# Small steps of each variance's root on ScalarE, VectorE or GpSimd, under a new written-out order

## The chip, the cores and the metric

The kernel runs on one core of one Trainium2 chip. The metric is the time of one execution in device microseconds. Five engines work side by side and run their own instructions in order: TensorE (PE) multiplies matrices into PSUM, VectorE (DVE) and ScalarE (ACT) work on SBUF and PSUM, GpSimd (POOL) works on SBUF only, and SyncE (SP) issues transfers that 16 DMA engines carry out. They meet through semaphores.

## The reference

Four layers act on one sequence of 2048 rows of 512 numbers, an attention layer (A) and a mixer (B), twice each with the same weights:

```python
x = x + A(layernorm(x), wqkv, wo)
x = x + B(layernorm(x), w1, w2, w3, w4)
x = x + A(layernorm(x), wqkv, wo)
x = x + B(layernorm(x), w1, w2, w3, w4)

def layernorm(x):                       # eps = 1e-5
    m, v = mean(x), var(x)              # over the 512 columns
    return (x - m) / sqrt(v + eps)
```

`A` has 32 heads of 16 columns; each row attends to 8 rows: itself and those 2, 4, ... 14 rows before it, with a softmax over the 8. `B` computes `h = gelu(layernorm(x) @ w1)`, shifts the four quarters of the columns of `h` by +1, -1, +2 and -2 rows, sets `x1 = x + shifted @ w2`, and returns `x1 + gelu(layernorm(x1) @ w3) @ w4` with a hidden width of 1792. Every layer norm needs, for each row, the reciprocal of a root of the variance: `r = (v + eps) ** -0.5`, and the shift `-m * r`.

## The kernel before, in words

**Tiles.** 128 rows are one tile, four tiles one block of 512 rows, and there are four blocks. Two layer pairs (attention and mixer) times four blocks make eight steps, n = 0 to 7. A step has stages, each a function that adds operations to a graph: `p1_quarters` and `p1_stream` (norm of x, product with wqkv, keys and values out to HBM; line 846), `p2` (attention; line 1021), `p3` (product with wo, residual, norm, product with w1, gelu; line 1148), `p4` (product with w2, norm of x1; line 1278) and `p5` (products with w3 and w4; line 1341). Products are made from pairs of f16 numbers (a high and a low half), as three f16 matmuls each, so a 128x512 product over 512 columns is a group of twelve matmuls. The low halves (`f<-f,f` in the profile, "turn" functions at lines 684 and 696) are made by VectorE or GpSimd, then a transposing transfer puts the tile in place for the next product.

**The root.** The sum of a tile's rows comes out of the instruction that makes the tile. `sq_dev` (line 651, ScalarE) squares the deviations and sums them into `ss`, 128 numbers, one a row. `power` (line 657) then issues three instructions on GpSimd, each on 128x1 numbers, through `stepped` (line 667): a first step `ve = ss * c1 + c2`, the power `r = ve ** -0.5`, and a last step `nb = (tot * c) * r`. In the profile all of these carry the name `small`: the first and the last are GpSimd's TENSOR_SCALAR `small<-small`, the power is its TENSOR_TENSOR `small<-small,nhalf`. `normed` (line 675) then applies `x * r + nb` as one ScalarE activation (in some tiles GpSimd does it); it appears as `f<-x,small`, `f<-f,small` and the like. `p1_norm` (line 750) has a form of the same three steps for the first block, and `p3` one with four steps (lines 1200 to 1205) on the roots of four tiles at once. In all there are 92 calls of `power`, 4 tiles of the first block, and 8 roots over four tiles.

**The order.** Nothing is left to the order in which the functions run. Every operation of the graph gets its place from a printed list, `PLACES` (line 56), and its engine, where it has more than one alternative, from a printed list `OTHER` (line 205). `plan` (line 278) goes through the operations by place, keeps along the way an estimate of the time at which each engine, transfer lane and buffer comes free, and gives each new tile the buffer that by this estimate is free first. Each engine then executes its instructions strictly in that order (line 354, which is why all rows of the profile name L354).

Of the kernel before, what the change touches and what calls it, by code (L numbers as in the profile page):

```python
# [12 lines left out]
ALU = mybir.AluOpType  # L13
# [214 lines left out]
class Graph:  # L228
# [3 lines left out]
    def __call__(self, key, alts, r=(), w=(), after=(), xfer=0.0, late=0.0):  # L232
# [34 lines left out]
        return o  # L267


LAT, LAT_PE, LAT_SP, LAT_DMA, LEAD, TABLE, COLD = 0.06, 0.35, 0.15, 1.5, 0.85, 1.3, 1.0  # L270
TAIL = (0.165, 0.085, 0.115, 0.0, 0.0)
FREE = (6.5, 1.0, 0.72, 1.2, 0.72)
LANES = 8
GRANT, HELD, SMALL = 0.14, 0.4, ("tiny", "root")
BY_DMA = {"p1": 1, "p2": 1, "p3": 1, "p4": 0}


# [1182 lines left out]
```

## Time and profile before

| | |
|---|---|
| median of 3 runs | 1149.2 us (1148.75 to 1150.22) |
| the profiled execution | 1149.52 us |
| its span, first to last instruction | 1147.7 us |
| mean granted TensorE clock | 0.995 |
| TensorE busy | 98% of the span |
| VectorE busy | 77% |
| ScalarE busy | 54% |
| GpSimd busy | 43% |

A row of the profile names the source line, the engine, the operation, output and inputs by the program's names, partitions and elements, and the count. In a timeline the first two numbers are start and length in microseconds, and brackets hold the idle time of that engine before the instruction and what ended it. In a list of groups the two numbers behind the first bar are the total in microseconds and the mean in nanoseconds of one. The busy time of TensorE includes matmuls that run at a lower granted clock.

### The profile page before, as it was taken

The page shows a single profiled execution, that of the slowest core. Times are in us where ns is not written, and L with a number is a line of the kernel's source. Part 1 is how long each engine was busy: PE and PEld are TensorE (multiplying, and loading weights), DVE is VectorE, ACT ScalarE, POOL GpSimd, SP SyncE. Part 2 cuts the span into 40 slices and gives each one's busy share as a digit, 9 for nine tenths or more (in the row PEclk, how much of TensorE's full clock was granted, in tenths as well). Part 3 has the DMA queues.
Part 4 walks back from the last instruction along what each step waited for, and adds up shares of the span by engine and source line. Part 5 has one row for each costly group of instructions (what it writes and reads, how often), then busy time and mean ns, then how long its engine had stood idle before and what let it go on. Part 6 is the DMA issues. An engine that isn't in the chain of part 4 may idle for free.

```text
span 1147.7 us, 15205 instructions
## 1 busy us (share of the span) xinstructions
PE 1121.6 (98%) x5236; PEld 526.5 (46%) x5236; DVE 880.8 (77%) x914; ACT 617.6 (54%) x1077; POOL 489.9 (43%) x619
## 2 busy tenths in 40 slices
PE   8999998998999999999999899999999999999998
PEld 6554444443444444444444344444444444444544
DVE  3999999988998998887889787777877989423212
ACT  4975884257754476365554556463545545545322
POOL 4656584156423455255535323444545342324000
PEclk9999999999999999999999899999999999999999
DMA  7789999998988579974488649884767567434323
GB/s 221 192 215 230 244 260 252 239 219 221 241 230 205 116 193 204 243 195 119 108 218 201 158 112 243 197 211 126 170 175 208 154 152 188 110 83 83 102 83 101
DMA packets 247101, 207.16 MB, mean 180 GB/s; under 512 B 134344, under 2 KB 188616, under 8 KB 247024
## 3 DMA queue, kind: packets, MB, share of 16 engines
q1 hardware_dynamic: 245408, 204.42, 71.2%
q10 hardware_dynamic: 1616, 1.77, 0.5%
q8 instruction: 41, 0.67, 0.3%
q14 instruction: 36, 0.29, 0.1%
HBM read 132.64 MB, written 37.87 MB: 149 GB/s over the span
## 4 chain that ended last, share of the span: by engine, by line
PE 55%; DVE 18%; POOL 8%; issue 7%; ACT 6%; DMA 5%; SPq 1%; POOLq 0%; DVEq 0%; ACTq 0%
PE mm L354 38%; PE acc L354 17%; DVE prod L354 10%; POOL small L354 4%; DVE L L354 3%; ACT f L354 2%; ACT junk L354 1%; SPq L354 1%; DMA kv<-kv_d 1%; DVE x L354 1%; POOL f L354 1%; DVE f L354 1%; DVE mx L354 1%; DVE g L354 1%; DMA w<-in_A_x_dram 1%
## 5 line engine op out<-in xcount | busy, mean ns | idle before, releaser
L354 PE MATMUL acc<-w,g 128*128 128x512 f16 (+1 forms) x1260 | 308.3, 393 | 2.0 <-DVE g L354 0.5
L354 PE MATMUL mm<-nT,w 128*128 128x512 f16 (+1 forms) x1344 | 293.5, 372 | 2.1 <-DVE g L354 1.1
L354 PE MATMUL mm<-wq_hl,xt 128*128 128x512 f16 x1008 | 230.4, 384 | 10.3 <-ACT f L354 3.4
L354 PEld LDWEIGHTS <-w 128*128 128x128 f16 x1512 | 141.2, 98 | 158.6 <-issue 7.3
L354 POOL TENSOR_SCALAR small<-small 128x1 f32<-128x1 f32 (+1 forms) x204 | 120.2, 590 | 158.2 <-ACT junk L354 147.0
L354 ACT ACTIVATE mm<-mm,s_w 128x512 f32<-128x512 f32 (+1 forms) x144 | 90.0, 627 | 174.3 <-PE mm L354 173.9
L354 PEld LDWEIGHTS <-g 128*128 128x128 f16 x1176 | 114.5, 98 | 140.4 <-DVE g L354 2.7
L354 DVE TENSOR_TENSOR prod<-kv,L 128x2048 f32<-128x2048 f32 x64 | 150.0, 2344 | 14.6 <-POOL o L354 10.3
L354 PEld LDWEIGHTS <-xt 128*128 128x128 f16 x1008 | 99.2, 99 | 132.3 <-issue 14.7
L354 DVE TENSOR_REDUCE L<-prod 128x128 f32<-128x2048 f32 x64 | 146.0, 2282 | 1.1
L354 DVE TENSOR_TENSOR prod<-kv,q 128x2048 f32<-128x2048 f32 x58 | 139.6, 2407 | 4.2 <-DMA kv<-kv_d 2.6
L354 DVE TENSOR_TENSOR prod<-prod 128x1024 f32<-128x1024 f32 (+1 forms) x114 | 121.5, 1068 | 5.3 <-ACT prod L354 2.8
L354 DVE SCALAR_TENSOR_TENSOR g<-mm,c_g,g 128x512 f16<-128x512 f32 x56 | 41.5, 746 | 78.2 <-ACT g L354 78.1
L354 PE MATMUL mm<-nT,w_hl 128*128 128x512 f16 x384 | 87.2, 380 | 1.8 <-DVE mx L354 1.8
L354 PE MATMUL mm<-w_hl,h 128*128 128x512 f16 x384 | 86.1, 379 | 0.4 <-POOL h L354 0.2
L354 POOL TENSOR_TENSOR g<-f,g 128x512 f16<-128x512 f32 x31 | 48.6, 1569 | 84.7 <-ACT f L354 42.0
L354 PE MATMUL mm<-wo_hl,oT 128*128 128x512 f16 x336 | 74.2, 379 | 0.0
L354 POOL TENSOR_TENSOR small<-small,nhalf 128x1 f32<-128x1 f32 (+1 forms) x104 | 71.1, 684 | 6.3
L354 POOL TENSOR_TENSOR prod<-prod 128x512 f32<-128x512 f32 x17 | 23.9, 1408 | 104.6 <-DVE prod L354 104.6
L354 ACT ACTIVATE g<-mm,c_g 128x512 f16<-128x512 f32 x98 | 66.5, 684 | 2.0
L354 PEld LDWEIGHTS <-oT 128*128 128x128 f16 x426 | 41.4, 98 | 50.4 <-DVE oT L354 1.2
L354 PEld LDWEIGHTS <-w_hl 128*128 128x128 f16 x384 | 37.6, 99 | 48.0 <-issue 4.2
(196 smaller groups left out, 1253.3 us busy)
## 6 DMA issues: line engine op xcount, KB each, us to landing
w<-w SPq DMA_DIRECT2D x210, 256.0 KB
kv<-kv_d SPq DMA_DIRECT2D x112, 352.0 KB
kv_d<-ev SPq DMA_DIRECT2D x112, 128.0 KB
w<-in_B_w_dram SPq DMA_DIRECT2D x42, 256.0 KB
q_d<-ev SPq DMA_DIRECT2D x28, 256.0 KB
w<-g SPq DMA_DIRECT2D x28, 256.0 KB
q<-q_d SPq DMA_DIRECT2D x28, 256.0 KB
x<-x SPq DMA_DIRECT2D x26, 256.0 KB
```

What stands on the lines that cost most here:

```text
L354: i = f(*a, **k).ins
```

## The change

`stepped` is gone. The three steps of `power` become four operations, and three of these have two alternatives each:

- a new step `tc = tot * C0` (GpSimd or ScalarE), which needs only the sum of the tile;
- the first step `ve = ss * c1 + c2` through a new function `affine` (ScalarE with a bias tile, or GpSimd);
- the power, always on GpSimd;
- the last step `nb = tc * r` (ScalarE or GpSimd).

The form in `p1_norm` gets the same alternatives for its first and last step, without `tc`. The root over four tiles in `p3` has three steps instead of four: the first on ScalarE or GpSimd, the power on GpSimd, the last, which now uses the four `tc`, on GpSimd or VectorE. Three constants for the bias are written by VectorE at the start, and the tile of small numbers grows from 288 to 336 columns.

Both printed lists are new. `OTHER` names 311 operations instead of 137, `PLACES` orders 3597 operations instead of 3513. `plan` no longer estimates times: it goes through the operations by place and gives each new tile the buffer that was returned first in that order.

```diff
 def plan(ops, slots):
-    free, latest = list(FREE), {}
-    lane, lanes = 0, [0.0] * LANES
-    pool = {k: [(0.0, j) for j in range(len(v))] for k, v in slots.items()}
+    pool = {k: list(range(len(v))) for k, v in slots.items()}
+    order = sorted(ops, key=lambda o: o.key)
...
-                got = min(pool[b.kind])
-                pool[b.kind].remove(got)
-                begin, b.slot = max(begin, got[0]), got[1]
+                b.slot = pool[b.kind].pop(0)
...
-                pool[b.kind].append((latest[b] + LAT, b.slot))
+                pool[b.kind].append(b.slot)
...
+    epss = const.tile([P, 3], F32, name="epss")
+    eps_of = {c: epss[:, k:k + 1] for k, c in enumerate((EPS, EPS / SN ** 2, EPS ** 2 / SN ** 2))}
+    for c, t in eps_of.items():
+        V.memset(t, c)
...
-    def power(key, ss, ve, r, i, c1, c2, tot, c, nb, k=None, j=None):
+    def power(key, ss, ve, r, i, c1, c2, tot, tc, nb, k=None, j=None):
         s, k, j = slice(i, i + 1), i if k is None else k, i if j is None else j
-        stepped(key, [
-            (0.21, lambda: G.tensor_scalar(ve.t[:, s], ss.t[:, j:j + 1], c1, c2, ALU.mult, ALU.add), [(ss, j)], [(ve, i)]),
-            (0.58, lambda: G.tensor_tensor(r.t[:, s], ve.t[:, s], nhalf[:, :1], ALU.pow), [(ve, i)], [(r, i)]),
-            (0.27, lambda: G.tensor_scalar(nb.t[:, s], tot.t[:, k:k + 1], r.t[:, s], c, ALU.mult, ALU.mult),
-             [(tot, k), (r, i)], [(nb, i)])])
-    def stepped(key, steps):
-        for k, (d, fn, r, w) in enumerate(steps):
-            gp(key, d, fn, r, w, cls="root" if k == len(steps) - 1 else "tiny")
+        op(key, [(POOL, 0.21, lambda: G.tensor_scalar(tc.t[:, s], tot.t[:, k:k + 1], C0, None, ALU.mult), "tiny"),
+                 (ACT, 0.25, lambda: A.activation(tc.t[:, s], tot.t[:, k:k + 1], AF.Copy, scale=C0), None)],
+           [(tot, k)], [(tc, i)])
+        affine(key, 1, ve, s, lambda: ss.t[:, j:j + 1], c1, c2, [(ss, j)], [(ve, i)])
+        gp(key, 0.58, lambda: G.tensor_tensor(r.t[:, s], ve.t[:, s], nhalf[:, :1], ALU.pow), [(ve, i)], [(r, i)], cls="tiny")
+        op(key, [(ACT, 0.25, lambda: A.activation(nb.t[:, s], tc.t[:, s], AF.Copy, scale=r.t[:, s]), None),
+                 (POOL, 0.27, lambda: G.tensor_scalar(nb.t[:, s], tc.t[:, s], r.t[:, s], None, ALU.mult), "root")],
+           [(tc, i), (r, i)], [(nb, i)])
+    def affine(key, n, ve, s, src, c1, c2, r, w):
+        bias = eps_of[c2]
+        op(key, [(ACT, 0.25, lambda: A.activation(ve.t[:, s], src(), AF.Identity, bias=bias, scale=c1), None),
+                 (POOL, 0.21, lambda: G.tensor_scalar(ve.t[:, s], src(), c1, c2, ALU.mult, ALU.add), "tiny")], r, w)
...
-        stepped(key + 0.2, [
-            (0.21, lambda: G.tensor_scalar(ve1.t[:, s4], ss.t[:, s4], C1, EPS, ALU.mult, ALU.add), [(ss, tiles)], [ve1]),
-            (1.04, lambda: G.tensor_tensor(r1.t[:, s4], ve1.t[:, s4], nhalf, ALU.pow), [ve1], [(r1, tiles)]),
-            (0.22, lambda: G.tensor_tensor(nb1.t[:, s4], sums.t[:, s4], r1.t[:, s4], ALU.mult),
-             [(sums, tiles), (r1, tiles)], [(nb1, tiles)]),
-            (0.23, lambda: G.tensor_scalar(nb1.t[:, s4], nb1.t[:, s4], C0, None, ALU.mult), [], [(nb1, tiles)])])
+        affine(key + 0.2, NT, ve1, s4, lambda: ss.t[:, s4], C1, EPS, [(ss, tiles)], [ve1])
+        gp(key + 0.2, 1.04, lambda: G.tensor_tensor(r1.t[:, s4], ve1.t[:, s4], nhalf, ALU.pow), [ve1], [(r1, tiles)], cls="tiny")
+        op(key + 0.2, [(POOL, 0.22, lambda: G.tensor_tensor(nb1.t[:, s4], tc.t[:, s4], r1.t[:, s4], ALU.mult), "root"),
+                       (DVE, 0.17, lambda: V.tensor_mul(nb1.t[:, s4], tc.t[:, s4], r1.t[:, s4]), None)],
+           [(tc, tiles), (r1, tiles)], [(nb1, tiles)])
```

The numbers such as 0.21 or 0.58 in these lines are the estimates that `plan` used before; in the changed kernel nothing reads them.

More of the change, by code (lines that the diff above doesn't have):

```diff
@@ L267, in __call__ @@
         return o
[L270 to L274, printed above, removed]
 BY_DMA = {"p1": 1, "p2": 1, "p3": 1, "p4": 0}
 def plan(ops, slots):
-    free, latest = list(FREE), {}
-    lane, lanes = 0, [0.0] * LANES
-    pool = {k: [(0.0, j) for j in range(len(v))] for k, v in slots.items()}
-    for o in ops:
+    pool = {k: list(range(len(v))) for k, v in slots.items()}
@@ L285, in plan @@
+    order = sorted(ops, key=lambda o: o.key)
+    for o in order:
         for kind, j in o.lend:
-            pool[kind].remove((0.0, j))
-    dma_free, port, wide, table, order = 0.0, 0.0, 0.0, None, []
-    for o in sorted(ops, key=lambda o: o.key):
+            pool[kind].remove(j)
+    for o in order:
         assert o.n == 0, "an operation stands before one that it needs"
-        e, d, o.fn, cls = o.alts[OTHER.get(o.seq, 0)]
-        begin = o.est
+        o.fn = o.alts[OTHER.get(o.seq, 0)][2]
@@ L292, in plan @@
         for b in o.touch:
             if b.slot is None:
-                got = min(pool[b.kind])
-                pool[b.kind].remove(got)
-                begin, b.slot = max(begin, got[0]), got[1]
+                b.slot = pool[b.kind].pop(0)
                 b.t = slots[b.kind][b.slot]
-        begin = max(begin, free[e])
-        if o.xfer:
-            begin = max(begin, *(lanes[(lane + k) % LANES] for k in range(o.parts)))
-            free[e] = begin + d
-            dma_free = max(dma_free, begin + d + LEAD) + o.xfer
-            o.end = dma_free + LAT_DMA + o.late
-            for k in range(o.parts):
-                lanes[lane] = o.end
-                lane = (lane + 1) % LANES
-        else:
-            if e == ACT and cls is not None and cls != table:
-                table = cls
-                d += TABLE
-            if e == POOL:
-                if begin < port:
-                    begin = max(begin, port - GRANT)
-                wide = max(wide, begin) if cls in SMALL else begin + d - GRANT
-            elif cls == "lock":
-                begin = max(begin, wide)
-                port = begin + d
-            if e == PE and begin - free[PE] > COLD and begin > 20.0:
-                d += min(begin - free[PE] - COLD, 2.5)
-            o.end = begin + d + (TAIL[PE] if e == PE else 0.0)
-            free[e] = o.end - TAIL[e]
-            if cls == "root":
-                o.end += HELD
@@ L324, in plan @@
-        order.append(o)
         for s in o.succ:
-            g = s.alts[0][0]
-            s.est = max(s.est, o.end + (LAT if e == g else LAT_PE if g == PE else LAT_SP if g == SP else LAT))
             s.n -= 1
         for kind, j in o.lend:
-            pool[kind].append((o.end + LAT, j))
+            pool[kind].append(j)
         for b in o.touch:
-            latest[b] = max(latest.get(b, 0.0), o.end)
             b.left -= 1
             if b.left == 0:
-                pool[b.kind].append((latest[b] + LAT, b.slot))
+                pool[b.kind].append(b.slot)
@@ L414, in keep @@
         return Buf(None, const.tile(shape, dt, name=name))
-    small, used = const.tile([P, 288], F32, name="small"), [0]
+    small, used = const.tile([P, 336], F32, name="small"), [0]
     def few(n):
         used[0] += n
-        assert used[0] <= 288
+        assert used[0] <= 336
         return Buf(None, small[:, used[0] - n:used[0]])
@@ L647, in tile_mixer @@
     stat = {ph: [[few(n) for k in range(SC)] for j in range(m)]
-            for ph, m, n in (("a", 5, NT), ("b", 8, NT), ("c", 5, NT + 1))}
+            for ph, m, n in (("a", 6, NT), ("b", 9, NT), ("c", 6, NT + 1))}
     x_sum = [few(NT) for b in range(NB)]
@@ L753, in p1_norm @@
         x = xs[0, b, i] if l else xin[0, b, i]
-        tot, ss, ve, r, nb = [s[n % SC] for s in stat["a"]]
+        tot, ss, ve, r, nb, tc = [s[n % SC] for s in stat["a"]]
         src = lambda: x.t if l else f32v(x.t, D)
         xr = (x, [0, 1]) if n == 0 and i < 2 else x
-        k = SN ** -2 if n else 1.0
+        k, eps = (SN ** -2, EPS / SN ** 2) if n else (1.0, EPS)
         if l == 0 and b >= STATS:
@@ L763, in p1_norm @@
             sq_dev(key, src, t, ss, i, [x])
-            power(key, ss, ve, r, i, C1 * k, EPS * k, t, C0, nb)
+            power(key, ss, ve, r, i, C1 * k, eps, t, tc, nb)
         else:
@@ L772, in p1_norm @@
             s = slice(i, i + 1)
-            stepped(key, [
-                (0.21, lambda: G.tensor_scalar(ve.t[:, s], mvt.t[:, 1:2], k, EPS * k, ALU.mult, ALU.add), [(mvt, 1)], [(ve, i)]),
-                (0.58, lambda: G.tensor_tensor(r.t[:, s], ve.t[:, s], nhalf[:, :1], ALU.pow), [(ve, i)], [(r, i)]),
-                (0.25, lambda: G.tensor_scalar(nb.t[:, s], r.t[:, s], DH ** -0.5, None, ALU.mult), [(r, i)], [(nb, i)])])
+            affine(key, 1, ve, s, lambda: mvt.t[:, 1:2], k, eps, [(mvt, 1)], [(ve, i)])
+            gp(key, 0.58, lambda: G.tensor_tensor(r.t[:, s], ve.t[:, s], nhalf[:, :1], ALU.pow), [(ve, i)], [(r, i)], cls="tiny")
+            op(key, [(ACT, 0.25, lambda: A.activation(nb.t[:, s], r.t[:, s], AF.Copy, scale=DH ** -0.5), None),
+                     (POOL, 0.25, lambda: G.tensor_scalar(nb.t[:, s], r.t[:, s], DH ** -0.5, None, ALU.mult), "root")],
+               [(r, i)], [(nb, i)])
         nr, xt = Buf("f32"), Buf(kind)
@@ L1151, in p3 @@
         key = n - 1.0
-        sums, ss, ve, r12, ve1, r1, nb, nb1 = [s[n % SC] for s in stat["b"]]
+        sums, ss, ve, r12, ve1, r1, nb, nb1, tc = [s[n % SC] for s in stat["b"]]
         n1_st[n] = r1, nb1
@@ L1186, in p3 @@
             sq_dev(key, src, sums, ss, i, [x])
-            power(key, ss, ve, r12, i, C1 * (1 + EPS) / SN ** 2, EPS ** 2 / SN ** 2, sums, C0, nb)
+            power(key, ss, ve, r12, i, C1 * (1 + EPS) / SN ** 2, EPS ** 2 / SN ** 2, sums, tc, nb)
             nr = Buf("f32")
@@ L1283, in p4 @@
             x2T[n].append(Buf("xt"))
-        sums, ss, ve, r, nb = [s[n % SC] for s in stat["c"]]
+        sums, ss, ve, r, nb, tc = [s[n % SC] for s in stat["c"]]
         for k, (m, i) in enumerate(group(n)):
@@ L1306, in p4 @@
             sq_dev(key, lambda x1=x1: x1.t, sums, ss, k, [x1])
-            power(key, ss, ve, r, k, C1 / SN ** 2, EPS / SN ** 2, sums, C0, nb)
+            power(key, ss, ve, r, k, C1 / SN ** 2, EPS / SN ** 2, sums, tc, nb)
             normed(key, nr, lambda x1=x1: x1.t, r, nb, k, [x1])
```

316 rows, old and new, of tables (OTHER, PLACES) are left out of this document.

## Prediction
> **What bounds the kernel now.** I read first the page's busy times, then TensorE's waits in order of time, then the granted clock around those waits, then the chain of waits leading into them.
>
> ```profile
> span 1147.7 us, 15205 instructions
> PE 1121.6 (98%) x5236; PEld 526.5 (46%) x5236; DVE 880.8 (77%) x914; ACT 617.6 (54%) x1077; POOL 489.9 (43%) x619
> ```
>
> TensorE is busy for 1121.6 of 1147.7 us, so 26.1 us is all its idle time. The change adds and removes no matmul: a gain can only come out of TensorE's holes and out of what a slow clock does behind them. The timeline of TensorE shows the largest holes away from both ends of the run; the number in brackets is the idle time, then who ended it.
>
> ```profile
> 176.79 7.04 PE L354 MATMUL mm<-wq_hl,xt 128*128 128x512 f16 x24 [2.38 <-DMA xt<-f]
> 184.86 6.01 PE L354 MATMUL mm<-nT,w 128*128 128x384 f16 x36 [1.02 <-ACT ev L354]
> 267.54 10.52 PE L354 MATMUL mm<-nT,w_hl 128*128 128x512 f16 x48 [1.62 <-DVE mx L354]
> 445.02 5.34 PE L354 MATMUL mm<-wq_hl,xt 128*128 128x512 f16 x24 [1.74 <-ACT ev L354]
> 638.98 5.28 PE L354 MATMUL mm<-wq_hl,xt 128*128 128x512 f16 x12 [3.36 <-ACT f L354]
> ```
>
> Two of them cost more than they show. The windows view (its last three columns: granted TensorE clock, DMA share, GB/s) has:
>
> ```profile
> 175.00:200.00 25.00, 22.18 (x98) 11.00 (x99) 24.38 (x17) 11.45 (x18) 9.33 (x9) 0.93 0.95 261
> 635.00:640.00 5.00, 1.64 (x6) 0.59 (x5) 4.28 (x6) 4.93 (x8) 1.00 (x1) 0.80 0.76 157
> 640.00:645.00 5.00, 5.00 (x13) 1.72 (x12) 4.77 (x3) 1.43 (x3) 0.79 (x2) 0.52 0.26 52
> ```
>
> After the 2.38 us hole the clock takes (1 - 0.93) x 25 = 1.75 us more; after the 3.36 us hole 5 x 0.20 + 5 x 0.48 = 3.4 us. So the five holes are worth 2.38 + 1.75 = 4.1, 1.0, 1.6, 1.7 and 3.36 + 3.4 = 6.8 us: 15.2 us together. Ahead of four of them the chain of waits (start, length, what) has a small GpSimd step of a variance's root that took 1 to 2.8 us:
>
> ```profile
> 174.56 2.67 POOL small L354
> 259.16 2.54 POOL small L354
> 440.38 1.06 POOL small L354
> 627.07 2.80 POOL small L354
> ```
>
> and ScalarE, which runs its queue in order, waits there for GpSimd:
>
> ```profile
> 177.26 0.81 ACT L354 ACTIVATE f<-f,small 128x512 f32<-128x512 f32 x1 [1.50 <-POOL small L354]
> 261.72 0.81 ACT L354 ACTIVATE f<-x,small 128x512 f32<-128x512 f32 x1 [3.08 <-POOL small L354]
> 440.33 0.81 ACT L354 ACTIVATE f<-prod,small 128x512 f32<-128x512 f32 x1 [1.32 <-POOL small L354]
> 442.92 0.81 ACT L354 ACTIVATE f<-f,small 128x512 f32<-128x512 f32 x1 [1.11 <-POOL small L354]
> ```
>
> The timeline at the largest hole shows why the step is slow:
>
> ```profile
> 614.75 1.31 POOL L354 TENSOR_SCALAR small<-small 128x1 f32<-128x1 f32 x1 [6.73 <-ACT junk L354]
> 619.48 0.55 POOL L354 TENSOR_TENSOR small<-small,nhalf 128x1 f32<-128x1 f32 x1
> 620.13 2.37 POOL L354 TENSOR_SCALAR small<-small 128x1 f32<-128x1 f32 x1
> 620.14 2.31 DVE L354 TENSOR_TENSOR prod<-kv,q 128x2048 f32<-128x2048 f32 x1
> 629.89 0.81 ACT L354 ACTIVATE f<-x,small 128x512 f32<-128x512 f32 x1 [3.43 <-POOL small L354]
> 638.25 0.68 ACT L354 ACTIVATE f<-mm,c_g 128x512 f32<-128x512 f32 x1
> ```
>
> The third step at 620.13 ends when VectorE's product ends (both near 622.5 us). ScalarE stands in its queue behind the roots for 3.43 us, so its later reads of PSUM come late; the one at 638.25 frees the bank for which TensorE waits until 638.98. The hole at 176.79 is of another kind: a normalized tile's low half was late on GpSimd, and its transpose went out only behind other transfers.
>
> ```profile
> 164.69 3.28 POOL L354 TENSOR_TENSOR f<-f,f 128x512 f16<-128x512 f32 x1
> 170.60 1.30 SPq L354 DMA_TRANSPOSE xt<-f  x1
> ```
>
> **The root, step by step.** Over the whole run the groups and the tile's spread (min/median/max ns) are:
>
> ```profile
> L354 POOL TENSOR_SCALAR small<-small 128x1 f32<-128x1 f32 x188 | 114.8, 612 | 155.6 <-ACT junk L354 145.3
> L354 POOL TENSOR_TENSOR small<-small,nhalf 128x1 f32<-128x1 f32 x96 | 58.3, 608 | 6.1
> L354 POOL TENSOR_SCALAR small<-small x204: 192/267/7862, 12.9 to 1052.4; 128x1 f32<-128x1 f32 x94, 128x4 f32<-128x4 f32 x8
> L354 POOL TENSOR_TENSOR small<-small,nhalf x104: 541/551/3133, 7.6 to 1051.8; 128x1 f32<-128x1 f32 x96, 128x4 f32<-128x4 f32 x8
> ```
>
> A free first step takes 0.19 us, a free last one 0.27; their mean is 0.61, so about 0.38 us of each is stall. The power in the middle means 0.61 against a median of 0.55: 0.06 of stall. A root costs 0.61 + 0.61 + 0.61 = 1.83 us now.
>
> By the lists in the diff, 52 of the 96 one-tile roots get their first step on ScalarE, 39 their last; the 92 new steps that scale the total beforehand split 46 to 46; of the eight four-tile roots three first steps go to ScalarE, three last ones to VectorE. That is 140 small instructions more on ScalarE. The trace of before has no one-element activation; the nearest rows are
>
> ```profile
> L354 ACT ACTIVATE g<-mm,c_g 128x512 f16<-128x512 f32 x98 | 66.5, 684 | 2.0
> L354 ACT ACTIVATE oT<-mm,c_g 128x128 f16<-128x128 f32 x14 | 4.9, 366 | 0.6 <-ACT mm L354 0.3
> L354 ACT ACTIVATION_READ_ACCUMULATOR junk<-x,small 128x1 f32 x38 | 7.1, 187 | 0.0
> ```
>
> It lies between 0.19 (the one-element read) and 0.37 us. The slope is (684 - 366) / 384 = 0.83 ns an element, so one element costs 366 - 127 x 0.83 = 0.26 us, which I take: 140 x 0.26 = 36 us on ScalarE. The lists also take 14 wide operations off it; ScalarE ends near 617.6 + 36 - 14 x 0.68 = 644 us, 56% of the span, which is no bound. The waiting that a last step on ScalarE does for the power is the waiting that the normalizing activation right behind it does now (the 3.08 and 3.43 us above); what queues behind is the same. A root with both outer steps on ScalarE costs 0.26 + 0.61 + 0.26 = 1.13 us if the power keeps its 0.06 of stall, 1.45 if it takes over the 0.38: 0.4 to 0.7 us less. GpSimd goes from 320 small steps to 261.
>
> [...]
>
> **The five holes.** Which slow step leaves GpSimd is read off the two lists (the order in which the roots' steps were issued, matched to the rows):
> - 638.98: of the three late steps that at 614.75 (a first one, 1.31 instead of 0.19) and that at 627.07 (a last one, 2.80 instead of 0.27) go to ScalarE, that at 620.13 stays. At stake 6.8, bounds 0 and 6.8; 1.1 + 2.5 of 5.7 us of stall goes, more than the hole's 3.36, and with a shorter hole the slow clock goes too: I take 5.0.
> - 267.54: the step at 259.16 (last) moves; its 2.3 us of stall is in the 3.08 us above, the hole is 1.6: I take 1.4, bounds 0 and 1.6.
> - 184.86: the step at 174.56 (last) moves; 2.4 us of stall for a hole of 1.0: I take 0.7, bounds 0 and 1.0.
> - 445.02: the slow step before 440.33 (last) stays, the one at 440.38 (first) moves: I take 0.6, bounds 0 and 1.7.
> - 176.79: no root's step stands in its way. Its low half stays on GpSimd; in the new order of transfers the loads of keys and values come before that half is ready, not between it and its transpose. I take 1.5, bounds 0 and 4.1.
>
> Sum of gains: 5.0 + 1.4 + 0.7 + 0.6 + 1.5 = 9.2 us, bounds 0 and 15.2.
>
> **What the new order gives back.** TensorE's order is nearly kept: counted in groups of twelve matmuls, which the timeline prices so:
>
> ```profile
> 325.65 2.75 PE L354 MATMUL acc<-w,g 128*128 128x512 f16 x12
> 328.24 2.10 PE L354 MATMUL mm<-nT,w 128*128 128x512 f16 x9
> ```
>
> (328.24 - 325.65 = 2.59 us a group), the work between the last matmul with wo and the first with w1, which covers the roots of one step, loses one group at steps 0, 2 and 4 and gains one at 3 and 5. A root chain (four tiles in a row) gets 0.4 to 0.7 us shorter a root, which nearly pays for one group. Bounds: 0, and 3 x 2.59 = 7.8 us if no chain gets shorter. I take one group of the three: +2.6 us.
>
> The rest I cost at nothing. Wide work moved between VectorE and GpSimd:
>
> ```profile
> L354 DVE TENSOR_TENSOR prod<-prod 128x512 f32<-128x512 f32 x48 | 35.8, 747 | 1.1
> L354 DVE TENSOR_TENSOR f<-f,f 128x512 f16<-128x512 f32 x29 | 20.1, 695 | 19.3 <-ACT f L354 19.0 <-issue 0.2
> L354 POOL TENSOR_TENSOR f<-f,f 128x512 f16<-128x512 f32 x24 | 35.0, 1460 | 19.1 <-ACT f L354 19.0
> ```
>
> Nine partial sums of attention come to VectorE (+9 x 0.75 at most = 6.7), twelve low halves go to GpSimd (-12 x 0.70 = -8.3): VectorE, at 77%, stays where it is. GpSimd drops 59 x 0.61 = 36 us and takes 16 wide operations, at most 16 x 1.46 = 23: it gets no busier. SP issues the same 774 groups of transfers in a much changed order; its price lies between nothing and, at the far end, the idle time that transfers end now, of which the 2.38 above is the most. Three memsets at the start, behind one of
>
> ```profile
> L354 DVE MEMSET nhalf<- x1: 62/62/62, 0.9 to 0.9; 128x4 f32 x1
> ```
>
> cost 0.06 us each on a VectorE that waits for the first input; without that cover, 0.2 us.
>
> The profiled execution took 1149.5 us for its 1147.7 of span, 0.3 above the median shown. 1149.5 - 9.2 + 2.6 = **1142.9 us**.
>
> **Rivals.**
> - *The stall only changes its victim*, and a root saves nothing where it counts: the power issues into VectorE's products and waits them out. For it: 0.38 of stall a step has to land somewhere. Against: the step at 620.13 was caught right behind its own power, and that place in the queue is gone where the last step moved. Gains 0, no group lost: 1149 us.
> - *The order takes the cover away* (slower): at steps 0, 2 and 4 the first w1 matmul comes one group earlier, and the chains aren't shorter there because step 4 keeps the stalled step at 620.13. The other holes still shrink (-4.2), that at 638.98 doesn't, and 7.8 comes on top: 1149.5 - 4.2 + 7.8 = 1153 us. It decides once a chain is shortened by less than 1.6 us. For it: the 2.38 us hole also cost 1.75 us of clock, so small holes are dear. Against: steps 3 and 5 get more cover.
> - *All goes well*: the five holes close, nothing is given back, 1149.5 - 15.2 = 1134 us.
>
> **Chances.** Forecast 0.57, changed victim 0.16, cover lost 0.19, all well 0.08. The forecast's own range is 1137 to 1147 (gains of 5 to 12.5, up to 2.6 given back); to hold 8 in 10 it must reach to both outer cases: 1135 to 1152. This measurement tells 0.2%, 2.3 us, from no change. Faster: 0.57 + 0.08, less a little for the forecast's upper edge: 0.64; slower 0.20; same 0.16.
>
> **What would show it.** Right: TensorE's idle time falls below 22 us; no stretch with a granted clock under 0.9 between 50 and 1100 us; the small TENSOR_SCALAR group of GpSimd shrinks from 188 to at most 147 with a lower mean; small activations at 0.2 to 0.37 us. The power's mean tells the first rival: near 0.61 it is dead, at 0.9 or more it holds. Wrong: a hole of over 2 us in front of matmuls with w1 (second rival), or ScalarE's waits for GpSimd no shorter while TensorE's holes are only elsewhere.

## The result and the profile after

The changed kernel takes 1131.6 us (1131.04 to 1132.07, 4 runs) against 1149.0 us of the kernel before in the same comparison: a ratio of 0.985, with a 95% interval of 0.983 to 0.987. It is faster by 17.4 us; 6.6 us were forecast. The profiled execution took 1131.96 us. The head of its page:

```profile
span 1130.2 us, 15220 instructions
PE 1115.9 (99%) x5236; PEld 528.2 (47%) x5236; DVE 877.4 (78%) x919; ACT 634.9 (56%) x1202; POOL 489.9 (43%) x577
```

TensorE's idle time fell from 26.1 to 1130.2 - 1115.9 = 14.3 us, and its busy time by 5.7 us. Of the latter, 3.0 us lie in the matmuls that the kernel before ran between 618 and 650 us, 6.8 us of that time at half clock; the rest is spread in small amounts and I don't explain it. Behind 110 us its timeline has one hole of over 0.75 us left, and the window around it still shows a slow clock:

```profile
182.38 7.69 PE L324 MATMUL mm<-nT,w 128*128 128x384 f16 x36 [2.89 <-DMA nT<-prod]
```

```profile
175.00:200.00 25.00, 22.11 (x90) 10.77 (x89) 24.59 (x18) 8.65 (x13) 12.29 (x9) 0.93 0.96 244
```

The five holes that the prediction names are gone. One of 2.89 us has opened between the places of the first two, with the same 0.93 of clock that the window had before. The small steps and ScalarE's waits for them (from the groups and the list of waits; a wait's three numbers are its sum, its count and the longest) in the changed kernel:

```profile
L324 POOL TENSOR_SCALAR small<-small 128x1 f32<-128x1 f32 x143 | 73.4, 516 | 61.5 <-ACT junk L324 30.8 <-DVE x L324 11.3 <-ACT small L324 10.7
L324 POOL TENSOR_TENSOR small<-small,nhalf 128x1 f32<-128x1 f32 x96 | 67.6, 705 | 70.8 <-ACT small L324 67.6
L324 ACT ACTIVATE small<-small 128x1 f32<-128x1 f32 x85 | 19.5, 235 | 23.7 <-POOL small L324 12.3 <-DVE f L324 6.4 <-DVE x L324 2.9
L324 ACT ACTIVATE small<-small,epss 128x1 f32<-128x1 f32 x52 | 15.1, 291 | 1.1
```

```profile
ACT small L324 <- POOL small L324: 12.3, 12, 2.5
ACT f L324 <- POOL small L324: 9.3, 8, 3.0
ACT prod L324 <- POOL small L324: 4.1, 5, 1.6
```

and the two largest such waits of the kernel before:

```profile
ACT f L354 <- POOL small L354: 46.6, 28, 5.0
ACT prod L354 <- POOL small L354: 9.7, 4, 3.0
```

ScalarE's waiting for small steps fell from 46.6 + 9.7 and two single waits of 3.9 and 2.8, 63 us in all, to 12.3 + 9.3 + 4.1 = 26 us. The power got slower (mean 705 ns instead of 608): it took over a part of the stall.

To see where the time went, I set the start of TensorE's first, second, ... last matmul in one trace against that in the trace of before. The table has what each stretch of the kernel before became shorter by, in us, for the changed kernel and the experiments that are told below (a minus is a loss). It is worked out from one profile each, and in places it carries up to 2 us of chance: e9 changes nothing ahead of 618 us but three memsets, and shows 1.4 and 1.0 us there; e12 differs from the changed kernel only at one step near 255 us, and shows 3.5 instead of 1.4 us ahead of that. Much of this is the slow clock: one piece of it costs 1.7 us (last section).

| stretch of before | after | e1 | e5 | e6 | e9 | e10 | e11 | e12 | e13 | e14 |
|---|---|---|---|---|---|---|---|---|---|---|
| 1 to 249 us | 1.4 | -10.4 | -0.8 | -0.2 | 1.4 | -0.4 | -0.7 | 3.5 | 0.9 | 0.8 |
| 249 to 281 | 4.0 | 0.2 | 4.1 | 1.8 | -0.2 | 4.0 | 3.4 | 0.7 | -0.2 | 4.1 |
| 281 to 437 | 2.4 | -7.3 | 0.0 | 0.6 | -0.7 | 0.0 | -0.3 | 2.4 | -5.6 | -0.7 |
| 437 to 465 | 3.0 | -5.2 | 0.1 | 0.1 | 1.0 | 1.1 | 0.0 | 2.6 | 2.9 | -0.9 |
| 465 to 618 | 0.3 | 0.3 | 0.0 | 0.1 | 0.0 | -0.4 | -0.4 | 0.3 | 0.3 | 0.0 |
| 618 to 650 | 6.4 | 6.4 | 2.2 | 2.6 | 4.0 | 5.3 | 0.2 | 6.4 | 6.4 | 1.3 |
| 650 to the end | 0.4 | -4.1 | 0.0 | 0.7 | -0.3 | -0.1 | 0.0 | 0.4 | 0.1 | 0.0 |

After 650 us nothing more is gained: 17.4 of the 17.8 us of the first column lie ahead of it.

### The profile page after: what moved, and what is told of

The parts are those of the page before. It is cut to its first block, busy times and chain, and to the rows that moved or that the text cites. A ratio compares the mean times of both kernels' runs of the same rounds, so it can differ in the third digit from the quotient of the medians.

```text
span 1130.2 us, 15220 instructions
## 1 busy us (share of the span) xinstructions
PE 1115.9 (99%) x5236; PEld 528.2 (47%) x5236; DVE 877.4 (78%) x919; ACT 634.9 (56%) x1202; POOL 489.9 (43%) x577
## 4 chain that ended last, share of the span: by engine, by line
PE 76%; DVE 12%; DMA 3%; ACT 3%; issue 3%; POOL 2%; SPq 1%; DVEq 0%; ACTq 0%; POOLq 0%
PE mm L324 53%; PE acc L324 24%; DVE prod L324 5%; DVE L L324 3%; DMA w<-in_A_x_dram 1%; POOL small L324 1%; ACT junk L324 1%; DVE g L324 1%; DMA kv_d<-ev 1%; SPq L324 1%; DVE mx L324 1%; DVE f L324 1%; ACT f L324 0%; DVE w_hl L324 0%; DVE h L324 0%
## 5 line engine op out<-in xcount | busy, mean ns | idle before, releaser
L324 PE MATMUL mm<-wq_hl,xt 128*128 128x512 f16 x1008 | 225.7, 379 | 1.9 <-DMA xt<-f 0.9
L324 DVE TENSOR_TENSOR prod<-kv,q 128x2048 f32<-128x2048 f32 x58 | 135.5, 2336 | 6.1 <-DMA kv<-kv_d 4.8
L324 DVE TENSOR_TENSOR prod<-prod 128x1024 f32<-128x1024 f32 (+2 forms) x118 | 129.5, 1102 | 2.9
L324 POOL TENSOR_TENSOR small<-small,nhalf 128x1 f32<-128x1 f32 (+1 forms) x104 | 78.3, 754 | 81.3 <-ACT small L324 78.0
L324 POOL TENSOR_SCALAR small<-small 128x1 f32<-128x1 f32 (+1 forms) x148 | 74.8, 508 | 62.0 <-ACT junk L324 30.8
L324 POOL TENSOR_TENSOR f<-f,f 128x512 f16<-128x512 f32 x31 | 49.0, 1582 | 34.8 <-ACT f L324 32.2
L324 PEld LDWEIGHTS <-h 128*128 128x128 f16 x384 | 37.7, 98 | 45.2 <-issue 0.6
```

The costliest lines, as they stand in the source:

```text
L324: i = f(*a, **k).ins
```

## The experiments

Each is timed against runs of the kernel before on the same chip; edits of the two printed lists are given in short form.

**Parts alone (e1 to e4).** The first theory was that the moved steps bring the gain (steps), the first rival that the new order does (order). e1 is the changed kernel with every small step back on GpSimd:

```diff
 OTHER = {int(k): 1 for k in """
...
-641 662 683 704 830 872 1052
...
+30 474 495 518 539 642 663
...
```

(49 numbers go and 94 come, those of the steps whose second alternative is GpSimd. The scaled totals are new steps, so GpSimd now runs 280 one-tile TENSOR_SCALAR `small<-small`, against 188 in the kernel before.)

> The changed kernel with its new lists of places, its wide engine choices and its buffer rule, but every small step of a root (first, last, scaled total) back on GpSimd; nothing is left out of the computation. Theory M (the gain of 17.4 us comes from small steps leaving GpSimd, which takes VectorE's products out of ScalarE's way): most of the gain goes, 1142 us or more, with holes of over 1 us in TensorE between 200 and 700 us. Theory O (the gain comes from the new order, and the steps could have stayed): at most 1136 us, and no new hole over 1 us behind 200 us. Between the two, both are needed.

Measured: 1168.2 us, ratio 1.018 (1.016 to 1.019). e2 is the changed kernel with the places and the wide engines of before, so that only the moved steps and the new buffer rule are left:

```diff
-PLACES = NEW_ORDER
+PLACES = OLD_ORDER
-OTHER = NEW_SMALL + NEW_WIDE
+OTHER = NEW_SMALL + OLD_WIDE
```

> The order of places of the kernel before and its wide engine choices, with the small steps on ScalarE, VectorE or GpSimd exactly as the change chose them (the scaled total stands right beside its square in the old order). Theory M: the holes at 267, 445 and 639 us shrink as the prediction had it, 1136 to 1143 us. Theory O: the old order keeps its holes, 1146 to 1151 us.

Measured: 1171.9 us, 1.021 (1.019 to 1.023). e3 is the changed kernel with only the engines of the wide operations put back:

```diff
-OTHER = NEW_SMALL + NEW_WIDE
+OTHER = NEW_SMALL + OLD_WIDE
```

> The changed kernel with the wide operations (low halves, partial sums, normalizations, weight halves) on the engines that the kernel before chose for them, all else as changed. If the wide choices were only a side effect: 1130 to 1134 us. If they carry part of the gain (fewer long GpSimd operations caught by VectorE's products): 1136 us or more. Theory M and theory O differ here only in that O allows the larger loss.

Measured: 1179.2 us, 1.027 (1.025 to 1.029). e4 is the kernel before with the new buffer rule:

```diff
-                got = min(pool[b.kind])
...
+                b.slot = pool[b.kind].pop(0)
```

> The kernel before with the new rule for buffers alone (the buffer returned first in the order, not the one estimated free first); no step moved, no order changed. Both theories: 1147 to 1151 us. If the rule matters by itself, it shows as more than 2.3 us either way.

Measured: 1163.8 us, 1.013 (1.011 to 1.015). The largest hole of e1 to e4, in this order:

```profile
424.46 10.47 PE L326 MATMUL mm<-wq_hl,xt 128*128 128x512 f16 x36 [5.02 <-DMA xt<-f]
```

```profile
192.06 8.21 PE L324 MATMUL mm<-nT,w 128*128 128x384 f16 x36 [5.29 <-DMA nT<-f]
```

```profile
874.53 4.02 PE L324 MATMUL acc<-w,g 128*128 128x512 f16 x10 [6.39 <-POOL g L324]
```

```profile
465.40 5.28 PE L319 MATMUL mm<-nT,w 128*128 128x512 f16 x12 [3.96 <-DVE g L319]
```

Each part alone is slower than both kernels. The order without the moved steps is not the cause by itself (e1), though e1 also loads GpSimd with 92 one-tile steps more than the kernel before had. e2 missed both expectations and can't be read for the steps, since the buffer rule that it carries costs 1163.8 - 1148.7 = 15 us under the old order by itself (e4, where I had expected no change).

**Five steps, all steps, and the buffer rule once more (e5 to e8).** The new theory was that the named steps count (named steps), its rival that order, engines and buffers hang together as a whole (fitted whole). e5 keeps everything of before, buffers too, and sends the five named small steps to ScalarE:

```diff
+MOVED = {1051, 1181, 1649, 2332, 2354}
...
+            if len(op.ops) in MOVED:
+                fn = act[0]
```

(`act[0]` is an activation with the same arithmetic.)

> The kernel before with its order, its engines for wide work and its buffers untouched; only the five small steps that the prediction's terms name (last steps at 174.56, 259.16 and 627.07, first steps at 440.38 and 614.75) go to ScalarE, a last one with its own scaling of the total right ahead of it. Named steps: their terms come whole, 5.0 + 1.4 + 0.7 + 0.6 = 7.7 us off 1149, 1141 us, and the holes ahead of 184.86, 267.54 and 638.98 shrink. Fitted whole: the five holes shrink or move, later queues of the old order meet at other times, and the time lies anywhere from 1145 to 1160 us with new holes elsewhere.

Measured: 1143.3 us, 0.996 (0.994 to 0.997), 5.0 us less than before, between the two expectations. Two holes of e5:

```profile
184.55 7.69 PE L369 MATMUL mm<-nT,w 128*128 128x384 f16 x36 [3.52 <-DMA nT<-f]
...
634.53 4.05 PE L369 MATMUL mm<-wq_hl,xt 128*128 128x512 f16 x12 [2.37 <-ACT f L369]
```

The table places the gain: 4.1 us between 249 and 281 us and 2.2 between 618 and 650. The hole at 267.54 is gone, the largest hole is only 1.0 us smaller, and that at 184.86 now waits for a transposing transfer. e6 does the same with all 94 outer steps that the change gives to ScalarE:

```diff
-MOVED = {1051, 1181, 1649, 2332, 2354}
+MOVED = FIRST_52 + LAST_39 + FOUR_TILES_3
```

> The kernel before with its order, its engines for wide work and its buffers untouched; all 94 outer steps that the change gives to ScalarE (52 first, 39 last, 3 of four tiles) go there, a first step right behind the squares that feed it, a last one right ahead of the first reader. Steps first: a root gets 0.4 to 0.7 us shorter everywhere and the time falls to 1135 to 1142 us. Fitted whole: without the order made for them the steps bring nothing, 1148 to 1165 us.

Measured: 1143.5 us, 0.996 (0.995 to 0.998). ScalarE's waits in e6:

```profile
ACT f L372 <- POOL small L372: 12.2, 11, 3.5
ACT small L372 <- POOL small L372: 6.2, 5, 2.1
ACT prod L372 <- POOL small L372: 4.8, 3, 2.4
```

With one wait of 4.3 us that is not listed here this makes 27 us, about the 26 of the changed kernel, and still the other 89 steps bring nothing beyond the five; this too lies between the two expectations. Most of the waiting that they take away was not what TensorE waited for. e7 is the changed kernel with the five steps back:

```diff
 OTHER = {int(k): 1 for k in """
+... 1068 ... 1203 ... 1685 ... 2384 ... 2408 ...
```

> The changed kernel with those same five steps back on GpSimd and nothing else touched. Named steps: the terms come back whole, 1131.6 + 7.7 = 1139 us, with holes of 1 to 3.4 us near 185, 267, 445 and 639 us. Fitted whole: each of the five costs only where it now meets a long VectorE product, a part of that or nothing, 1131.5 to 1136 us.

Measured: 1134.8 us, 0.988 (0.987 to 0.990). Against the kernel before on its own chip it saves 13.5 us, 3.9 less than the changed kernel. The hole of 2.89 us has grown to 4.39 us, and a new one is

```profile
277.38 5.35 PE L325 MATMUL mm<-wq_hl,xt 128*128 128x512 f16 x24 [2.47 <-DMA xt<-prod]
```

and between 618 and 650 us it keeps the whole 6.4 us, counted as in the table. So in the changed kernel the named steps are not what closed the largest hole. e8 is the changed kernel with the buffer rule of before:

```diff
+                got = min(pool[b.kind])
...
-                b.slot = pool[b.kind].pop(0)
```

> The changed kernel with the buffer rule of before, which gives the buffer that is free first by estimated times; order and engines are the new ones. Buffers don't matter with this order: 1131 to 1134 us. Fitted whole: as the new rule under the old order cost 15 us, so the old rule under the new order costs 5 to 20 us, 1137 to 1152 us, with ScalarE, VectorE or transfers waiting for another owner of their buffer.

Measured: 1132.6 us, 0.987 (0.986 to 0.989), an interval that overlaps with that of the changed kernel; the profiled spans are 1130.0 and 1130.2 us. With the new order the buffer rule makes no difference that can be told (1 or 2 us aren't excluded), and under the old one it costs 15 us.

**One exponential, one small step (e9 to e12).** What closed the largest hole? In the timeline of ScalarE before, ahead of the read at 638.25 that frees the bank, stands:

```profile
633.73 1.28 ACT L354 ACT_TABLE_LOAD   x1
635.02 0.63 ACT L354 ACTIVATE L<-L 128x512 f32<-128x512 f32 x1
635.67 1.28 ACT L354 ACT_TABLE_LOAD   x1
```

The softmax's exponential with a table load on either side takes 3.24 us (633.73 to 636.97), behind the wait of 3.43 us for GpSimd. In the changed kernel the slow small steps (with the VectorE product that overlaps the last of them), and the same three, are

```profile
606.33 1.32 POOL L324 TENSOR_TENSOR small<-small,nhalf 128x1 f32<-128x1 f32 x1 [3.69 <-ACT small L324]
609.78 2.69 POOL L324 TENSOR_SCALAR small<-small 128x1 f32<-128x1 f32 x2
616.88 2.50 POOL L324 TENSOR_TENSOR small<-small,nhalf 128x1 f32<-128x1 f32 x1
616.67 2.28 DVE L324 TENSOR_TENSOR prod<-kv,q 128x2048 f32<-128x2048 f32 x1
```

```profile
615.68 1.28 ACT L324 ACT_TABLE_LOAD   x1
616.97 0.63 ACT L324 ACTIVATE L<-L 128x512 f32<-128x512 f32 x1
622.82 1.28 ACT L324 ACT_TABLE_LOAD   x1
```

The stalls are still there (2.69 for two steps, 2.50 for a power), but the exponential lies among the roots, where ScalarE waits for GpSimd in any case (1.56 us ahead of 613.15 and 1.23 ahead of 619.41). e9 makes that one change in the kernel before; all small steps stay on GpSimd:

```diff
+EXP_AT, EXP_FIRST = 1862, (2355, 2144, 2145, 2365, 2356, 2366)
...
+    for k, q in enumerate(EXP_FIRST):
+        at[q] = at[EXP_AT] + 0.05 * (k + 1)
```

(Operation 1862 is the exponential; the six that stood ahead of it on ScalarE follow it.)

> The kernel before with all small steps on GpSimd, same engines and buffers; one change in ScalarE's queue: the softmax's exponential at 635.02, which brings two table loads (633.73 and 635.67), goes ahead of the normalizing activation at 629.89, where ScalarE stands idle waiting for GpSimd anyway. Steps of the root are the cause at 638.98: the stalls are all still there, so the hole stays and the time is 1148 to 1150 us. ScalarE's queue is the cause: the bank is freed some 2 us earlier (3.24 us of exponential and loads gone from in front of it, one load of 1.28 back), the hole shrinks from 3.36 to about 1.4 us and the slow clock behind it goes: 1143.5 to 1146 us, all of it gained between 618 and 650 us.

Measured: 1145.1 us, 0.997 (0.996 to 0.998). Its ScalarE and the hole:

```profile
624.94 1.28 ACT L383 ACT_TABLE_LOAD   x1
626.24 0.63 ACT L383 ACTIVATE L<-L 128x512 f32<-128x512 f32 x1
628.36 0.81 ACT L383 ACTIVATE f<-x,small 128x512 f32<-128x512 f32 x1 [1.49 <-POOL small L383]
629.19 1.28 ACT L383 ACT_TABLE_LOAD   x1
```

```profile
635.50 2.75 PE L383 MATMUL mm<-wq_hl,xt 128*128 128x512 f16 x12 [1.42 <-ACT f L383]
```

The hole shrank from 3.36 to 1.42 us (1.4 expected), 12 matmuls behind it take 2.75 us instead of 5.28, and the stretch gained 4.0 us without one small step moved (a hole of 0.70 us, ended by VectorE, opens behind). e10 adds the exponential's move to e5:

```diff
 MOVED = {1051, 1181, 1649, 2332, 2354}
+EXP_AT, EXP_FIRST = 1862, (2355, 2144, 2145, 2365, 2356, 2366)
```

> The five steps of before on ScalarE and the exponential moved as well. If the two causes at the largest hole are separate, the rest of that hole (2.37 us with the five steps moved) closes too and the stretch from 618 to 650 us gains the changed kernel's 6.4 us instead of 2.2: 1139 to 1140 us. If they are the same time counted twice: 1142 to 1144 us.

Measured: 1141.9 us, 0.994 (0.993 to 0.996), between the two expectations; the hole is gone, one of 0.85 us for a transposing transfer stands behind it, and the stretch gained 5.3 us of the changed kernel's 6.4. The gains of this stretch hold pieces of slow clock of up to 1.7 us each, which come or stay away by where a hole falls (last section); the holes tell more: the five steps shorten the hole of 3.36 by 1.0 us, the exponential by 1.9, both together close it. By this stretch the two causes are nearly separate (2.2 + 4.0 = 6.2). By the medians, each against its own runs of before, e10 saves 7.0 us and e5 5.0: the move adds 2.0 us there, and 3.8 alone (e9), so the sum is not a clean one. e11 moves a single small step, the last one at 259.16:

```diff
+MOVED = {1181}
```

> The kernel before with one small step moved, the last step at 259.16. If that step alone carries the gain of the five between 249 and 281 us (4.07 us there): 1144 to 1145.5 us. By the prediction's term for it 1.4 us: 1147 us. If the five only work together: 1148 to 1150 us.

Measured: 1146.3 us over 10 runs, 0.998 (0.997 to 0.998), 2.6 us less than before and between the first two expectations. In its timeline of TensorE the hole of 1.62 us is gone, the two behind it are smaller, and the large one stays:

```profile
276.51 2.75 PE L369 MATMUL mm<-wq_hl,xt 128*128 128x512 f16 x12 [0.74 <-DVE h L369]
279.92 2.75 PE L369 MATMUL mm<-wq_hl,xt 128*128 128x512 f16 x12 [0.65 <-DVE h L369]
...
636.69 5.28 PE L369 MATMUL mm<-wq_hl,xt 128*128 128x512 f16 x12 [3.11 <-ACT f L369]
```

against these in the kernel before:

```profile
263.10 2.81 PE L354 MATMUL acc<-w,g 128*128 128x512 f32 x6 [0.42 <-POOL small L354]
267.54 10.52 PE L354 MATMUL mm<-nT,w_hl 128*128 128x512 f16 x48 [1.62 <-DVE mx L354]
279.22 2.75 PE L354 MATMUL mm<-wq_hl,xt 128*128 128x512 f16 x12 [1.17 <-DVE h L354]
282.68 2.53 PE L354 MATMUL mm<-wq_hl,xt 128*128 128x512 f16 x11 [0.70 <-DVE h L354]
```

e12 puts the same step back in the changed kernel:

```diff
 OTHER = {int(k): 1 for k in """
+... 1203 ...
```

> The changed kernel with that one step back on GpSimd. If it carries the loss that the five brought: 1134 to 1135.5 us, with a hole of about 2.5 us near 277 us; if another of the five does: 1131.5 to 1132.5 us.

Measured: 1133.8 us, 0.987 (0.985 to 0.988). Against the kernel before on its own chip it saves 15.1 us, 2.3 less than the changed kernel, but the two intervals overlap. The traces are clearer: the gain of the stretch from 249 to 281 us falls from 4.0 to 0.7 us, with a hole that e7 has too:

```profile
275.06 5.35 PE L324 MATMUL mm<-wq_hl,xt 128*128 128x512 f16 x24 [1.59 <-DMA xt<-prod]
```

Of the five, this one step carries nearly all of the gain (3.4 of 4.1 us, e11 and e5) and of the loss in this stretch.

**Two halves (e13, e14).** Open was whether the other gains need each other. At about 305 us both orders have issued the same TensorE work; e13 joins the old first half to the new second half, e14 the new first to the old second:

```diff
-order = NEW
+order = OLD[:1220] + rest(NEW)
...
+order = NEW[:1220] + rest(OLD)
```

> Two halves joined at about 305 us, where both orders have issued the same TensorE work: the order, engines and small steps of the kernel before ahead of the cut, those of the changed kernel behind it; buffers by the rule of before. The traces put 5.5 us of the changed kernel's 17.4 us ahead of the cut and 11.9 behind it. If the gains sit where the traces show them and don't need each other: 1148.8 - 11.9 = 1137 us. If the order works only as one whole: nothing or a loss, 1145 to 1160 us.

> The same two halves the other way round: the changed kernel up to about 305 us, the kernel before behind it. If the gains are local: 1148.8 - 5.5 = 1143.3 us, with the hole of 3.4 us near 634 us back. If the order works only as one whole: 1146 to 1160 us.

Measured: e13 1145.0 us, 0.998 (0.997 to 0.999); e14 1144.3 us, 0.996 (0.995 to 0.998). The hole behind the cut in e13, and the largest one of e14:

```profile
321.24 7.83 PE L370 MATMUL mm<-nT,w 128*128 128x512 f16 x24 [5.16 <-DMA w<-w]
```

```profile
635.76 4.34 PE L373 MATMUL mm<-wq_hl,xt 128*128 128x512 f16 x12 [3.35 <-ACT f L373]
```

e14 came near what local gains would give (1143.3); its 1.3 us between 618 and 650 us are clock alone, since the hole stays and one piece of slow clock follows it instead of two. e13 missed its 1137 by 8 us, and the table shows where: it loses 6.6 us at the cut itself (the 5.16 us hole with a slow clock behind it, where the weights' transfers of one order meet the need of the other), and then repeats the changed kernel's gains, 2.9, 0.3 and 6.4 us. So the gains of the second half don't need the first half; an order needs its own transfers at the place where it starts.

## Why the prediction was wrong in its size

The direction was right; the sum of 9.2 less 2.6 us stands against 17.4. Even the bound of 15.2 for "all goes well" was too low: it counted five holes and the clock behind two of them. What each term came to:

- **638.98** (5.0 taken, bounds 0 to 6.8): 6.4 us came, but by another cause. The step that failed is "1.1 + 2.5 of 5.7 us of stall goes, more than the hole's 3.36". Moved alone, the named steps brought 2.2 us (e5) and all 94 brought 2.6 (e6): the step at 620.13 kept its stall (2.41 us in both), and the exponential stood where it was. With every small step back on GpSimd the new order still brought 6.4 (e1). The exponential and its two table loads, ahead of the bank's read, are worth 4.0 by themselves (e9). How much of the 6.4 their new place brings in the changed kernel isn't shown: there TensorE's own order differs too (48 matmuls with wo in a row from 606.96 us before, groups of twelve between other work after), and no run has the new order with the exponential in its old place. The chain of waits led me to the stall, and I read ScalarE's own queue only up to 629.89, not the 3.24 us between 633.73 and 636.97.
- **267.54** (1.4 taken, bound 1.6): 4.0 us between 249 and 281 us, 3.4 of it by the one step at 259.16 alone (e11). The mechanism was right and the term mis-sized: its bound was the hole of 1.62 us, but the ones of 0.42 us ahead of it and 1.17 us behind it weren't counted. They hang on the same step: with it moved the first is gone and the second falls to 0.74 us (e11).
- **445.02** (0.6 taken): the stretch from 437 to 465 us gained 3.0, but 0.1 with the named step moved (e5) or all of them (e6). So the named step doesn't bring it. The second half of the changed kernel does (2.9 in e13), with its order, engines and steps together; the order with all steps on GpSimd lost 5.2 us there (e1). The timelines of before and after show another run of matmuls with wq there:

```profile
430.17 13.11 PE L354 MATMUL mm<-wq_hl,xt 128*128 128x512 f16 x60
```

```profile
419.89 20.88 PE L324 MATMUL mm<-wq_hl,xt 128*128 128x512 f16 x96
```

  60 stood in a row before the hole, and 96 now; that this is the cause wasn't tried.
- **184.86 and 176.79** (0.7 and 1.5 taken): nothing beyond the table's chance (1.4 us up to 249 us). Both holes are gone, and one of 2.89 us for a transposing transfer stands there; in e5 the first hole was 1.71 and the second 3.52. It looks as if time saved at one hole of this chain of normalized tiles, low halves and transposes is waited out at the next; no run tries that.
- **What the new order gives back** (2.6 taken, bounds 0 to 7.8): nothing seen. No stretch of the table is lost, although one group of twelve matmuls fewer covers the roots at steps 0, 2 and 4. The second rival, with its hole in front of matmuls with w1, didn't come.
- **What I cost at nothing**: the new buffer rule had no term in the sum. In the changed kernel it makes no difference that can be told (e8), so this didn't hurt; under the old order it costs 15 us (e4). The wide operations that change engines were also at nothing, and they are fitted to the new order: put back, they cost 1179.2 - 1131.6 = 48 us (e3).
- **The first rival** (the stall changes its victim) is right in part. The power's mean went to 705 ns, between my two marks of 0.61 and 0.9 us; its stall above 0.55 us rose from about 5.6 to 15 us (96 times 0.058 and 0.155). The trace has such a stall beside a VectorE product: a power, 0.55 us at the median before, takes 2.50, from 616.88 to 619.38 us, while a product with two inputs runs from 616.67 to 618.95. Whether the product holds the power back, no run tried. Yet the time didn't stay where it was.
- **The signs**: idle time under 22 us came (14.3), the group of 188 became 143 with a lower mean (516 ns), and the small activations took 0.19 to 0.29 us for the 0.26 estimated. "No stretch with a granted clock under 0.9" failed at 180 to 190 us, where two windows of 5 us show 0.83.

Left open is the mechanism behind 437 to 465 us, and the 2.4 us between 281 and 437. In the latter the kernel before has two holes that the prediction doesn't name, 0.70 us at 282.68 and 1.07 us at 320.47; neither is left, and why wasn't tried.

## What to carry to other kernels

Where an in-order engine waits in its queue, list everything that stands between the wait and the instruction that the bottleneck needs: here one exponential with two table loads behind the wait was worth more than the stalls in front of it. Only a stall that ends a hole of the bottleneck counts: one moved step alone brought 2.6 us, all 94 brought 4.8. An order written out by hand and its engine choices must be tried together: taken apart (e1 to e4) the parts were 15 to 31 us slower than before, though the whole gained 17. What a part costs depends on the rest: the new buffer rule cost 15 us under the old order and nothing that can be told under the new.

## What the runs showed of the hardware

**The slow clock isn't a matter of the hole's length alone.** The same 36 matmuls near 183 us follow a hole in nearly every run. Here they are in e12, e8 and e9:

```profile
181.40 6.01 PE L324 MATMUL mm<-nT,w 128*128 128x384 f16 x36 [2.33 <-DMA nT<-prod]
```

```profile
180.53 7.70 PE L364 MATMUL mm<-nT,w 128*128 128x384 f16 x36 [2.38 <-DMA nT<-prod]
```

```profile
183.58 6.01 PE L383 MATMUL mm<-nT,w 128*128 128x384 f16 x36 [3.40 <-DMA nT<-f]
```

After 2.33 us and after 3.40 us they run at full speed (6.01), after 2.38 us they take 7.70 and lose 1.7 us. What differs is where the hole falls. In the clock records of all 16 traces the granted clock changes only on a grid of 3.41 us, and a stretch of half clock lasts one piece of it or two (3.41 or 6.83 us): in the kernel before from 177.21 to 180.62 and from 638.01 to 644.83, two starts that are 460.80 us or 135 pieces apart. One piece costs 3.41 x 0.5 = 1.7 us, the 7.70 less 6.01 us above. In windows along this grid (the first number behind the length is TensorE's busy time, the third from the right its clock), e8 has its hole inside one piece, and e9 has its longer one over two:

```profile
177.27:180.68 3.41, 1.03 (x6) 0.31 (x4) 3.41 (x3) 2.09 (x3) 3.41 (x2) 1.00 1.04 234
180.68:184.09 3.41, 3.41 (x12) 1.62 (x11) 3.34 (x3) 0.00 (x0) 2.09 (x2) 0.50 0.00 0
```

```profile
178.41:181.83 3.42, 1.78 (x9) 0.59 (x6) 3.18 (x3) 2.62 (x5) 2.91 (x3) 1.00 0.74 167
181.83:185.24 3.41, 1.66 (x11) 1.04 (x12) 3.38 (x2) 0.94 (x1) 0.00 (x0) 1.00 1.01 256
185.24:188.65 3.41, 3.41 (x23) 2.05 (x22) 3.34 (x3) 1.16 (x2) 0.00 (x0) 1.00 0.95 229
```

Over the 16 traces, of the pieces at full clock 34 had 2.05 us or more without a matmul, and half clock followed each of them; 5203 had less than 1.65 us, and half clock followed none. Between these, 4 of 17 were followed by half clock. An idle time of a whole piece wasn't needed: 2.05 us within one were enough each time. The grid starts at another place in each run (4.33 us in e9, 6.60 in e8). So the holes of 2.33 to 3.40 us shown here cost the matmuls behind them 0 or 1.7 us more by where they fell, and the one of 3.36 us at 638.98 in the kernel before, with two pieces, cost 2.9: the 24 matmuls behind it took 5.28 and 3.15 us for twelve instead of 2.75 (the 3.4 of the prediction counts the idle part of the slow clock too). Two profiles of nearly the same kernel can differ by such a piece, as e12's 6.01 and e8's 7.70 us do. What sets the clock isn't shown.

**A one-element activation** took 0.19 us with constants and 0.29 us with a pointer for its scale or bias (changed kernel, 0.185 at the least and 0.298 at the most); GpSimd's small step took 0.19 to 0.27 us in the kernel before when nothing stood in its way (least and median of 204), so moving it saves the stall and not the work.
